# Five moves of work beside a dense feed-forward loop: an earlier load, later norm factors, later kernel products, and column tiles in turns

## The chip, the cores and the metric

The kernel runs on one core of a Trainium2 chip. The metric is the time on the device in microseconds (us). The engines are TensorE (PE; PEld is its weight load), VectorE (DVE), ScalarE (ACT), GpSimd (POOL, which here mostly issues transfers on a queue of its own) and SyncE (SP, which issues the transfers of the feed-forward weights).

## The reference

A block with adaptive layer norm: a diagonal state space convolution (S4D) over 2048 tokens of 576 channels, then a dense feed-forward layer with ReLU.

```python
def _A_ref(u, ...):                       # L = 2048 tokens, D = 576 channels, N = 128 states
    dt = jnp.exp(log_dt)
    A = -jnp.exp(log_A_real) + 1j * A_imag
    C = (C_real + 1j * C_imag) * dt[:, None]
    P = jnp.exp((A * dt[:, None])[:, :, None] * pos[None, None, :])
    K = 2.0 * jnp.einsum("dn,dnl->dl", C, P).real
    y = irfft(rfft(u_t, 2 * L) * rfft(K, 2 * L), 2 * L)[:, :, :L]
    return y + u * D_skip

def _B_ref(x, w1, w2):                    # 576 -> 4608 -> 576
    return jnp.maximum(x @ w1, 0) @ w2

mod = (silu(c) @ w_mod)                   # sa, ca, ga, sb, cb, gb
h = layernorm(x) * (1 + ca) + sa
x = x + ga * _A_ref(h, ...)
h = layernorm(x) * (1 + cb) + sb
x = x + gb * _B_ref(h, w1, w2)
```

## The kernel before

The 2048 tokens are cut into four blocks of 512. The convolution of block s needs spectra of the channels (`U`) and of the convolution kernel (`K`) of every block up to s; `Ud`, `Rd` and `Kd` are copies of them in device memory, and `Ua`, `R`, `Ka` are tiles that are loaded from there. The channels are worked in two halves p = 0 and 1.

Up to about 213 us a prelude makes the first part of the convolution kernel and runs convolution 0. Then one loop, `ffn`, carries the program: 144 groups g, 36 for each block of tokens. A group is 14 matmuls `hps` (`first(g)`, line 1305) and, two groups behind, 14 matmuls `acc` (`second`, line 1330). Between them ACT writes `hh`, the ReLU, and DVE writes `hl`, what is left of it for a second pass (line 1311). `hps` has two buffers, so `first(g + 2)` waits for `hl` of g. In block 0 the weights are also split (`w`, on ACT and DVE) and kept for the later blocks.

All other work runs beside that loop. `step()` is called four times a group; each call takes a few items from the generator of the current block. An item that yields a number is DVE work of about so many us, `None` is PE work, and `-1` ends the step. Block 0's generator makes the rest of the convolution kernel (`rest`: rotations `rots` on DVE into `W1r`, then matmuls `products` into `kps`, line 440, from three-block products with 48 columns and one-block products with 16) and, alternating with it, the first norm of block 1, then convolution 1. Block 1's generator finishes block 0's output, makes what the rest of the kernel needs (`rest` again, with 32 columns) and runs convolution 2; block 2's runs convolution 3.

Convolution s is written as a list of pieces, some of them alternating by `both`: transform `U` (`mm_U`, `spec_U`), transform the kernel (`mm_K`, `spec_K`: a butterfly into K, then K2 from K and the loaded R), multiply (`product`: Y from K2 with `Ua`, the spectrum of block 0, and from R with the own U), transform back (`back`, `inverse` into `ps_i`), then `norm2` with transposes `ps_t`, whose results `xh`, `xl`, `xs` are what the next block's `first` reads. Evictions `oT` free the accumulators of the block before. `cps`, the PSUM tile of `kps`, `ps_f` and `ps_i`, has one buffer in this part; spectra share a ring of six (`spec`).

The final order on each engine is set by a scheduler from this order of issue; each engine then works in order. POOL's queue takes saves and loads in the order in which they stand, and an entry that waits holds all behind it. The norm's `norms` makes the roots (variance to standard deviation, on ACT) and right behind them reciprocals and products on DVE.

Of the kernel before, what the change touches and what calls it, by code (L numbers as in the profile page):

```python
# [46 lines left out]
class KGen:  # L47
# [335 lines left out]
    def rest(self, psum, items, beside=iter(())):  # L383


        nc, k = self.nc, self.k
# [3 lines left out]
        with ExitStack() as ctx:  # L390
# [37 lines left out]
            def products(h, W1, W2, blocks):  # L428
                na = 16 * len(blocks)
                key = (h // 6, blocks)  # L430
                if key not in kes:
                    kes[key] = pt.tile([P, na, 72], F32, name=f"ker_{h}")
                ke = kes[key]
                for half in range(2):
                    ps = psum.tile([P, 6, na], F32, tag="cps", bufs=1, name="kps")
                    for q in range(6):
                        for dd in range(4):
                            ch = dd * 12 + 6 * half + q
                            for r in range(2):
                                nc.tensor.matmul(  # L440
                                    ps[32 * dd : 32 * dd + 32, q, :],
                                    W2[:, r, :, ch],
                                    W1[:, :na, r, ch],
                                    start=(r == 0),
                                    stop=(r == 1),
                                )
                        if q == 2:
                            yield None
                    q0 = 12 * (h % 6) + 6 * half
                    nc.scalar.activation(  # L450
                        ke[:, :, q0 : q0 + 6], ps.rearrange("p q a -> p a q"), AF.Copy
                    )
                    yield None
                rows[key] = rows.get(key, 0) + 1
                if rows[key] == 6:
                    yield -1
                    for i, s in enumerate(blocks):
                        self.store(
                            s, h // 6, ke[:, 16 * i : 16 * i + 16].rearrange("p a q -> p (a q)"),
                            nc.gpsimd,  # L460
                        )

            nxt = load(items[0][0])
            yield -1
            prev = iter(())
            for i, (h, blocks) in enumerate(items):
                W2, W0, Z = nxt
# [19 lines left out]
class Body:  # L487
# [317 lines left out]

    def norms(self, st, kept):

        nc = self.nc
        rs = []
        for i in range(4):  # L810
            mv = self.sm.tile([P, 5], F32, tag="mv", bufs=4, name="mv")
            nc.vector.bn_aggr(out=mv[:, 0:2], in_=st[i])
            sq = nc.scalar.activation(mv[:, 2:3], mv[:, 1:2], AF.Sqrt, bias=self.eps)
            if kept:
                self.tc.keep_in_program_order(sq)
            else:
                self.kept(sq)
            rs.append(mv)
        for mv in rs:
            nc.vector.reciprocal(mv[:, 3:4], mv[:, 2:3])  # L820
            nc.vector.tensor_scalar(
                mv[:, 4:5], mv[:, 0:1], mv[:, 3:4], -1.0, op0=ALU.mult, op1=ALU.mult
            )
        return rs

    def sums(self, name):
        return [self.sm.tile([P, 2, 6], F32, tag="st", bufs=8, name=name) for _ in range(4)]
# [11 lines left out]
    def norm1(self, x2, h):  # L839

        f = self.nc.vector.scalar_tensor_tensor
        st = self.sums("st1")
        for p in range(2):
            yield from self.stats(
                lambda i: x2[:, i, p * PC : (p + 1) * PC], [t[:, p] for t in st]
            )
        rs = self.norms(st, False)
        yield 2.0
        for i in range(4):
            mv = rs[i]  # L850
            f(h[:, i], x2[:, i], mv[:, 0:1], self.m["ca"], op0=ALU.subtract, op1=ALU.mult)
            f(h[:, i], h[:, i], mv[:, 3:4], self.m["sa"], op0=ALU.mult, op1=ALU.add)
            yield 1.6

    def conv(self, s):
# [33 lines left out]
        def spec_K(p, Z):  # L889
            R = self.load(self.Rd[s - 1][p], "R")  # L890
            Rs.append(R)
            K = self.spec(f"K_{s}_{p}")
            yield from self.butterfly(Z, K, -1)
            yield -1
            if s + 1 < NB:
                self.save(self.Rd[s][p], K)
# [10 lines left out]

        def product(p, Y):
            def pair(t):
                if t == 0 or s == 1:  # L910
                    Ka = (Rs if t else Ks)[p]
                else:
                    Ka = self.load(self.Kd[s - t][p], "Ka")
                Ua = Us[p] if t == s else self.load(self.Ud[t][p], "Ua")
                return Ka, Ua

            order = [0, s, *range(1, s)]
            nxt = pair(0)
            yield -1
            for i, t in enumerate(order):  # L920
                Ka, Ua = nxt
                if i + 1 < len(order):
                    nxt = pair(order[i + 1])
                yield from self.product(Y, Ka, Ua, i == 0)

# [6 lines left out]
            yield from self.butterfly(Y, V, 1)  # L932
            Vs.append(V)

        Us, Ks, Rs, Vs = [], [], [], []
        if s == 1:
            ZU = self.spec("Z")
            yield from mm_U(0, ZU)
# [3 lines left out]
            yield from both(spec_U(1, Z1), mm_K(0, ZK))  # L942
            kt[1] = self.load_kt(s, 1)
            yield from spec_K(0, ZK)
            ZK = self.spec("Z")
            Y = self.spec(f"Y_{s}_0")
            yield from both(product(0, Y), mm_K(1, ZK))
        else:
            ZK = self.spec("Z")
            yield from both(self.norm1(x2, h), mm_K(0, ZK))  # L950
# [610 lines left out]
```

## Time and profile before

| | us |
|---|---|
| three runs | 1371.61, 1366.92, 1363.95 |
| median | 1366.92 |
| profiled execution: its span | 1360.4 |
| PE busy in it | 1226.0 |
| DVE busy | 871.4 |
| ACT busy | 503.5 |
| prelude, up to the first groups | 213 |

The profiled execution has no time of its own beside its span; the median stands 6.5 us above that span. Rows of the trace give a start, a duration, the engine, the line, the operation and the tiles as out<-in; a bracket behind a row is the time that the engine stood idle before it and what ended that idle time. Rows of waits give the engine and line that waited, what for, and the total in us, the number of times and the longest. Line numbers are those of the kernel before.

### The profile page before, as it was taken

What the parts mean: (1) busy time and instruction counts of PE and PEld (TensorE: products, weight loads), DVE (VectorE), ACT (ScalarE), POOL (GpSimd) and SP (SyncE); (2) the same over time, 40 slices, a digit from 0 to 9 for tenths busy, and PEclk for the clock granted to TensorE, in tenths of its full rate; (3) what the DMA queues carried; (4) which work ended last, traced back from release to release, by engine and by line L of the source; (5) the groups of instructions that cost most, each with busy time, mean ns of one, the idle gap of its engine ahead of it and who ended that gap; (6) DMA issues with size and microseconds to landing.
All of it is one profiled execution on the core that took longest, in us unless ns stands there. A gap on an engine that the chain in (4) does not pass through costs nothing.

```text
span 1360.4 us, 26053 instructions
## 1 busy us (share of the span) xinstructions
PE 1226.0 (90%) x10608; PEld 973.7 (72%) x10608; DVE 871.4 (64%) x1351; ACT 503.5 (37%) x1014; POOL 195.3 (14%) x271
## 2 busy tenths in 40 slices
PE   5125797999999987999999999999999999999998
PEld 3124565777787766777777887787888888888886
DVE  5978997998878698469737986266999222111111
ACT  7986234222224311622233225333322253233321
POOL 1777231111120100021101100100010000000000
PEclk9557899999999998999999999999999999999999
DMA  6666499988898755699689894677997567666651
GB/s 196 243 246 241 135 356 366 331 292 275 292 344 289 265 199 207 205 362 316 236 278 342 294 362 143 206 245 233 317 348 259 178 177 211 198 195 197 197 174 61
DMA packets 132424, 340.47 MB, mean 250 GB/s; under 512 B 22352, under 2 KB 22672, under 8 KB 132304
## 3 DMA queue, kind: packets, MB, share of 16 engines
q1 hardware_dynamic: 105200, 215.21, 48.9%
q0 software_dynamic: 26816, 123.01, 24.6%
q8 instruction: 83, 1.36, 0.4%
q10 hardware_dynamic: 288, 0.59, 0.1%
q14 instruction: 37, 0.30, 0.1%
HBM read 258.55 MB, written 80.22 MB: 249 GB/s over the span
## 4 chain that ended last, share of the span: by engine, by line
PE 70%; DVE 11%; DMA 10%; issue 4%; ACT 2%; POOL 1%; SPq 0%; DVEq 0%; ACTq 0%; POOLq 0%
PE acc L1330 28%; PE hps L1305 28%; PE kps L440 5%; PE ps_f L757 4%; PE kps L262 3%; DVE T L509 2%; DVE Y L509 2%; DMA Ua<-Ud 2%; DMA Ud<-U 2%; DVE k L133 1%; PE ps_i L998 1%; DMA h<-in_x_dram 1%; DMA Ka<-Rd 1%; DMA Zr<-Zd 1%; DMA W1d<-W 1%
## 5 line engine op out<-in xcount | busy, mean ns | idle before, releaser
L1330 PE MATMUL acc<-hh,w 128*128 128x512 f32 x1296 | 422.1, 400 | 0.3 <-DVE w L509 0.3
L1305 PE MATMUL hps<-xh,w 128*128 128x512 f32 x1152 | 394.3, 402 | 4.4 <-ACT xh L1061 3.5
L1311 DVE SCALAR_TENSOR_TENSOR hl<-hps,hh 128x512 fp32r<-128x512 f32 x144 | 99.0, 688 | 291.3 <-ACT hh L1310 291.0
L1330 PEld LDWEIGHTS acc<-hh,w 128*128 128x128 f32 x1296 | 242.1, 188 | 52.5 <-DVE w L509 0.9
L1330 PE MATMUL acc<-hl,w 128*128 128x512 f32 x720 | 278.7, 399 | 0.0
L1305 PEld LDWEIGHTS hps<-xh,w 128*128 128x128 f32 x1152 | 217.4, 190 | 52.1 <-ACT xh L1061 4.7
L1305 PE MATMUL hps<-xl,w 128*128 128x512 f32 x576 | 230.8, 401 | 0.2 <-DVE xl L1066 0.2
L1310 ACT ACTIVATE hh<-hps 128x512 fp32r<-128x512 f32 x144 | 86.0, 598 | 354.6 <-PE hps L1305 347.0
L1283 ACT ACTIVATE w<-r 128x576 fp32r<-128x576 f32 x144 | 98.6, 686 | 217.9 <-issue 168.4
L1330 PEld LDWEIGHTS acc<-hl,w 128*128 128x128 f32 x720 | 135.3, 188 | 28.2
L1305 PEld LDWEIGHTS hps<-xl,w 128*128 128x128 f32 x576 | 109.2, 190 | 24.8 <-DVE xl L1066 1.5
L1305 PE MATMUL hps<-xs,w 128*128 128x512 f32 x288 | 97.2, 417 | 14.3 <-DVE hl L1311 14.0
L1276 ACT ACTIVATE w<-r 128x640 fp32r<-128x640 f32 x142 | 104.0, 733 | 12.4 <-DMA r<-in_w_dram 12.4
L262 PE MATMUL kps<-W,W 128*32 128x16 f32 x2304 | 40.3, 215 | 71.5 <-POOL W L59 47.3
L262 PEld LDWEIGHTS kps<-W,W 128*32 128x32 f32 x2304 | 37.9, 150 | 76.2 <-POOL W L59 49.7
L440 PEld LDWEIGHTS kps<-W1r,W2r 128*32 128x32 f32 x3456 | 68.4, 146 | 30.7 <-issue 16.8
L509 DVE TENSOR_TENSOR Y<-Y,T 128x1152 f32<-128x1152 f32 x64 | 84.7, 1351 | 0.2
L440 PE MATMUL kps<-W1r,W2r 128*32 128x48 f32 (+2 forms) x3456 | 77.4, 238 | 7.0 <-DVE W1r L412 3.3
L1305 PEld LDWEIGHTS hps<-xs,w 128*128 128x128 f32 x288 | 52.8, 190 | 28.3 <-DVE hl L1311 17.1
L758 ACT ACTIVATE Z<-ps_f 128x288 f32<-128x288 f32 x104 | 42.4, 407 | 63.1 <-PE ps_f L757 62.3
L509 DVE TENSOR_TENSOR w<-r,w 128x512 fp32r<-128x512 f32 (+2 forms) x108 | 57.9, 572 | 8.6 <-ACT w L1283 8.6
L509 DVE TENSOR_TENSOR W<-Z 128x576 f32<-128x576 f32 x52 | 37.1, 752 | 29.3 <-ACT Z L758 29.3
(216 smaller groups left out, 1362.8 us busy)
## 6 DMA issues: line engine op xcount, KB each, us to landing
r<-in_w_dram SPq DMA_DIRECT2D x144, 320.0 KB, 4.2
r<-in_w_dram SPq DMA_DIRECT2D x144, 288.0 KB, 3.7
w<-L1d SPq DMA_DIRECT2D x108, 320.0 KB, 3.0
w<-L2d SPq DMA_DIRECT2D x108, 288.0 KB, 3.2
W2r<-W2d POOLq DMA_DIRECT2D x18, 1536.0 KB, 9.4
W2d<-W SPq DMA_DIRECT2D x10, 1536.0 KB, 7.4
W<-W1d POOLq DMA_DIRECT2D x18, 768.0 KB, 8.9
Ua<-Ud POOLq DMA_DIRECT2D x12, 1152.0 KB, 10.3
```

The costliest lines, as they stand in the source:

```text
L133: self.nc.vector.scalar_tensor_tensor(f[:, i].rearrange(pair, u=2), th, float(slot), k[:, i].rearrange(pair, u=2), op0=ALU.mult, op1=ALU.s ...
L262: self.nc.tensor.matmul(ps[32 * dd : 32 * dd + 32, 12 * u + q, :], W2[:, r, :, ch], W1[:, u, :, r, ch], start=(r == 0), stop=(r == 1),)
L440: nc.tensor.matmul(ps[32 * dd : 32 * dd + 32, q, :], W2[:, r, :, ch], W1[:, :na, r, ch], start=(r == 0), stop=(r == 1),)
L509: return self.kept(self.nc.vector.tensor_tensor(*args, **kw))
L757: kept(nc.tensor.matmul(o, fc[:, n2, c, :], src(n2), start=True, stop=True))
L758: nc.scalar.activation(Z[:, n2, c], ps[:, :PC], AF.Copy)
L1276: nc.scalar.activation(w[:, 0], r, AF.Copy)
L1283: nc.scalar.activation(w[:, 0:D], r2[g], AF.Copy)
L1305: nc.tensor.matmul(ps, a, x, start=(i == 0), stop=(i == 13))
L1310: nc.scalar.activation(hh, ps, AF.Relu)
L1311: nc.vector.scalar_tensor_tensor(hl, ps, 0.0, hh, op0=ALU.max, op1=ALU.subtract)
L1330: nc.tensor.matmul(acc[i], a, x, start=(f == 0 and j in (0, 3, 6, 9, 12)), stop=(f == NF - 1 and j in (2, 5, 8, 11, 13)),)
```

## The change

Five pieces. The matmuls of `products` go through the four column tiles for one half of the sum, then for the other, where they finished a column tile before the next. In block 1 `rest` ends five steps behind its first load, where it ended one. `norms` is split into `roots` and `factors`; `norm1` has its factors three steps behind the roots. In convolution 1 `Ua` is loaded between the two parts of K's butterfly and kept in a list for the product. Also there, `Y` is allocated ahead of the tile for the next transform of the kernel, and that transform starts three items later beside the product.

```diff
@@ -434,9 +434,9 @@
                 for half in range(2):
                     ps = psum.tile([P, 6, na], F32, tag="cps", bufs=1, name="kps")
                     for q in range(6):
-                        for dd in range(4):
-                            ch = dd * 12 + 6 * half + q
-                            for r in range(2):
+                        for r in range(2):
+                            for dd in range(4):
+                                ch = dd * 12 + 6 * half + q
                                 nc.tensor.matmul(
                                     ps[32 * dd : 32 * dd + 32, q, :],
                                     W2[:, r, :, ch],
@@ -461,7 +461,8 @@
                         )
 
             nxt = load(items[0][0])
-            yield -1
+            for _ in range(1 if most == 48 else 5):
+                yield -1
             prev = iter(())
             for i, (h, blocks) in enumerate(items):
                 W2, W0, Z = nxt
@@ -805,6 +806,12 @@
 
     def norms(self, st, kept):
 
+        rs = self.roots(st, kept)
+        self.factors(rs)
+        return rs
+
+    def roots(self, st, kept):
+
         nc = self.nc
         rs = []
         for i in range(4):
@@ -816,12 +823,16 @@
             else:
                 self.kept(sq)
             rs.append(mv)
+        return rs
+
+    def factors(self, rs):
+
+        nc = self.nc
         for mv in rs:
             nc.vector.reciprocal(mv[:, 3:4], mv[:, 2:3])
             nc.vector.tensor_scalar(
                 mv[:, 4:5], mv[:, 0:1], mv[:, 3:4], -1.0, op0=ALU.mult, op1=ALU.mult
             )
-        return rs
 
     def sums(self, name):
         return [self.sm.tile([P, 2, 6], F32, tag="st", bufs=8, name=name) for _ in range(4)]
@@ -844,8 +855,12 @@
             yield from self.stats(
                 lambda i: x2[:, i, p * PC : (p + 1) * PC], [t[:, p] for t in st]
             )
-        rs = self.norms(st, False)
-        yield 2.0
+        rs = self.roots(st, False)
+        yield 1.0
+        for _ in range(3):
+            yield -1
+        self.factors(rs)
+        yield 1.0
         for i in range(4):
             mv = rs[i]
             f(h[:, i], x2[:, i], mv[:, 0:1], self.m["ca"], op0=ALU.subtract, op1=ALU.mult)
@@ -890,7 +905,11 @@
             R = self.load(self.Rd[s - 1][p], "R")
             Rs.append(R)
             K = self.spec(f"K_{s}_{p}")
-            yield from self.butterfly(Z, K, -1)
+            W = self.spec("W")
+            yield from self.butterfly1(Z, W)
+            if s == 1:
+                Uas.append(self.load(self.Ud[0][p], "Ua"))
+            yield from self.butterfly2(W, K, -1)
             yield -1
             if s + 1 < NB:
                 self.save(self.Rd[s][p], K)
@@ -911,7 +930,9 @@
                     Ka = (Rs if t else Ks)[p]
                 else:
                     Ka = self.load(self.Kd[s - t][p], "Ka")
-                Ua = Us[p] if t == s else self.load(self.Ud[t][p], "Ua")
+                if t == s:
+                    return Ka, Us[p]
+                Ua = Uas[p] if s == 1 else self.load(self.Ud[t][p], "Ua")
                 return Ka, Ua
 
             order = [0, s, *range(1, s)]
@@ -932,7 +953,7 @@
             yield from self.butterfly(Y, V, 1)
             Vs.append(V)
 
-        Us, Ks, Rs, Vs = [], [], [], []
+        Us, Ks, Rs, Vs, Uas = [], [], [], [], []
         if s == 1:
             ZU = self.spec("Z")
             yield from mm_U(0, ZU)
@@ -942,9 +963,9 @@
             yield from both(spec_U(1, Z1), mm_K(0, ZK))
             kt[1] = self.load_kt(s, 1)
             yield from spec_K(0, ZK)
+            Y = self.spec(f"Y_{s}_0")
             ZK = self.spec("Z")
-            Y = self.spec(f"Y_{s}_0")
-            yield from both(product(0, Y), mm_K(1, ZK))
+            yield from both(product(0, Y), after(3, mm_K(1, ZK)))
         else:
             ZK = self.spec("Z")
             yield from both(self.norm1(x2, h), mm_K(0, ZK))
```

On POOL's queue in convolution 1: `Ud_1` is the save of U's second half, `kt` a load of the convolution kernel, `Rd` and `Kd` the saves of K and K2, `R` and `Ua` loads. Before:

```order
L748 DMA Ud_1_104<-U_1_5469 128x4x576
L1238 DMA kt<-kd_1_60 128x16x72
L748 DMA Rd_0_111<-K_0_5563 128x4x576
L748 DMA Kd_0_115<-K_1_0_5615 128x4x576
L744 DMA Ua<-Ud_0_101 128x4x576
L744 DMA R<-Rd_1_110 128x4x576
L748 DMA Rd_1_112<-K_1_5846 128x4x576
L744 DMA Ua<-Ud_1_102 128x4x576
L748 DMA Kd_1_116<-K_1_1_5909 128x4x576
```

and after:

```order
L749 DMA Ud_1_104<-U_1_5496 128x4x576
L745 DMA Ua<-Ud_0_101 128x4x576
L1259 DMA kt<-kd_1_60 128x16x72
L749 DMA Rd_0_111<-K_0_5595 128x4x576
L749 DMA Kd_0_115<-K_1_0_5644 128x4x576
L745 DMA R<-Rd_1_110 128x4x576
L745 DMA Ua<-Ud_1_102 128x4x576
L749 DMA Rd_1_112<-K_1_5865 128x4x576
L749 DMA Kd_1_116<-K_1_1_5923 128x4x576
```

The load of `Ua` for half 0 moved from behind the saves `Rd_0` and `Kd_0` to right behind `Ud_1`; for half 1 it moved ahead of the save `Rd_1`.

On DVE at the same place, where the product of half 0 begins (`Y_0`; `K_1_0` is K2; `w` are splits of the feed-forward weights). Before:

```order
L1311 SCALAR_TENSOR_TENSOR hl<-hps,hh 128x512
L509 TENSOR_TENSOR w_5661<-r_5625,w_5661 128x640
L509 TENSOR_TENSOR w_5702<-r_5571,w_5702 128x64
L509 TENSOR_TENSOR w_5702<-r_5571,w_5702 128x512
L509 TENSOR_TENSOR Y_0_5647<-K_1_0_5615,Ua 128x4x288 x2
L509 TENSOR_TENSOR T<-K_1_0_5615,Ua 128x1152 x2
L509 TENSOR_TENSOR Y_0_5647<-Y_0_5647,T 128x4x288 x2
L1311 SCALAR_TENSOR_TENSOR hl<-hps,hh 128x512
L509 TENSOR_TENSOR T<-R,U_0_5378 128x1152 x2
```

and after:

```order
L918 SCALAR_TENSOR_TENSOR K_1_0_5644<-R,sgn,K_0_5595 128x4x288
L920 SCALAR_TENSOR_TENSOR K_1_0_5644<-R,sgn,K_0_5595 128x4x288
L1332 SCALAR_TENSOR_TENSOR hl<-hps,hh 128x512
L510 TENSOR_TENSOR Y_0_5667<-K_1_0_5644,Ua 128x4x288 x2
L510 TENSOR_TENSOR w_5684<-r_5555,w_5684 128x64
L510 TENSOR_TENSOR w_5684<-r_5555,w_5684 128x512
L510 TENSOR_TENSOR w_5658<-r_5623,w_5658 128x640
L510 TENSOR_TENSOR T<-K_1_0_5644,Ua 128x1152
L1332 SCALAR_TENSOR_TENSOR hl<-hps,hh 128x512
L510 TENSOR_TENSOR Y_0_5667<-Y_0_5667,T 128x4x288
L510 TENSOR_TENSOR T<-K_1_0_5644,Ua 128x1152
```

The first product moved ahead of three weight splits, which now stand between its pieces, and an `hl` stands in the midst of it.

On ACT at the end of block 0's groups (`oT` and `o` evict the accumulators; `xf`, `xs`, `xh` are the input of block 1's groups). Before:

```order
L1416 ACTIVATE oT<-acc_0_3035,m_gb 128x512
L1061 ACTIVATE xh_6180<-xf 128x512
L1059 ACTIVATE xf<-ps_t,m_sb,m_cb 128x512
L1416 ACTIVATE oT<-acc_0_3036,m_gb 128x512
L1061 ACTIVATE xh_6180<-xf 128x512
L1059 ACTIVATE xf<-ps_t,m_sb,m_cb 128x512
L1061 ACTIVATE xh_6180<-xf 128x512
L1059 ACTIVATE xf<-ps_t,m_sb,m_cb 128x512
L1061 ACTIVATE xh_6180<-xf 128x512
L1310 ACTIVATE hh<-hps 128x512
L1276 ACTIVATE w_6392<-r_6364 128x640
L1310 ACTIVATE hh<-hps 128x512
```

and after:

```order
L1437 ACTIVATE oT<-acc_0_3035,m_gb 128x512
L1082 ACTIVATE xs_6189<-xf 128x512
L1437 ACTIVATE oT<-acc_0_3036,m_gb 128x512
L1437 ACTIVATE oT<-acc_0_3037,m_gb 128x512
L1080 ACTIVATE xf<-ps_t,m_sb,m_cb 128x512
L1437 ACTIVATE oT<-acc_0_3038,m_gb 128x512
L1082 ACTIVATE xh_6187<-xf 128x512
L1080 ACTIVATE xf<-ps_t,m_sb,m_cb 128x512
L1437 ACTIVATE o_6452<-acc_0_3039,m_gb 128x512
L1082 ACTIVATE xh_6187<-xf 128x512
L1080 ACTIVATE xf<-ps_t,m_sb,m_cb 128x512
L1304 ACTIVATE w_6470<-r_6366 128x576
```

All five evictions now stand ahead of the last `xh`, of which two more follow; two did before.

On DVE at block 1's start, where the rotations for the kernel's rest begin (`x_0` is block 0's output). Before:

```order
L1477 TENSOR_TENSOR x_0_2525<-ps_o_6535,x_0_2525 128x64
L1311 SCALAR_TENSOR_TENSOR hl<-hps,hh 128x512
L408 TENSOR_TENSOR T<-W_6_6567,Zr_6568 128x1536
L410 TENSOR_TENSOR W1r_6585<-W_6_6567,Zr_6568 128x1536
L412 TENSOR_TENSOR W1r_6585<-W1r_6585,T 128x16x48
L414 TENSOR_TENSOR W1r_6585<-W1r_6585,T 128x16x48
L1311 SCALAR_TENSOR_TENSOR hl<-hps,hh 128x512
L408 TENSOR_TENSOR T<-W1r_6585,Zr_6568 128x1536
L410 TENSOR_TENSOR W1r_6585<-W1r_6585,Zr_6568 128x1536
L412 TENSOR_TENSOR W1r_6585<-W1r_6585,T 128x16x48
L414 TENSOR_TENSOR W1r_6585<-W1r_6585,T 128x16x48
L1311 SCALAR_TENSOR_TENSOR hl<-hps,hh 128x512
```

and after:

```order
L1498 TENSOR_TENSOR x_0_2525<-ps_o_6535,x_0_2525 128x64
L1332 SCALAR_TENSOR_TENSOR hl<-hps,hh 128x512
L408 TENSOR_TENSOR T<-W_6_6567,Zr_6568 128x1536
L410 TENSOR_TENSOR W1r_6628<-W_6_6567,Zr_6568 128x1536
L412 TENSOR_TENSOR W1r_6628<-W1r_6628,T 128x16x48
L1332 SCALAR_TENSOR_TENSOR hl<-hps,hh 128x512
L414 TENSOR_TENSOR W1r_6628<-W1r_6628,T 128x16x48
L408 TENSOR_TENSOR T<-W1r_6628,Zr_6568 128x1536
L410 TENSOR_TENSOR W1r_6628<-W1r_6628,Zr_6568 128x1536
L412 TENSOR_TENSOR W1r_6628<-W1r_6628,T 128x16x48
L414 TENSOR_TENSOR W1r_6628<-W1r_6628,T 128x16x48
L1332 SCALAR_TENSOR_TENSOR hl<-hps,hh 128x512
```

The rotations come one `hl` later against block 0's output, and an `hl` stands within the first of them.

## The prediction

> **What bounds the kernel now.** I read the page first: its busy shares and the chain that ended last.
>
> ```profile
> span 1360.4 us, 26053 instructions
> PE 1226.0 (90%) x10608; PEld 973.7 (72%) x10608; DVE 871.4 (64%) x1351; ACT 503.5 (37%) x1014; POOL 195.3 (14%) x271
> PE 70%; DVE 11%; DMA 10%; issue 4%; ACT 2%; POOL 1%; SPq 0%; DVEq 0%; ACTq 0%; POOLq 0%
> ```
>
> TensorE (PE) carries the end. What can be won without fewer matmuls is its idle time, and time at a low clock. Second I read busy time by stretches: from 445 to 560 us convolution 1 runs beside block 0's last groups, to 620 block 1 starts, and behind 852 block 2.
>
> ```profile
> core 0: us, PE busy (x) PEld busy (x) DVE busy (x) ACT busy (x) POOL busy (x), PEclk, DMA share, GB/s
> 230.00:445.00 215.00, 209.60 (x2945) 163.39 (x2944) 187.89 (x232) 58.14 (x115) 30.53 (x46) 1.00 0.87 309
> 445.00:560.00 115.00, 102.29 (x421) 79.45 (x420) 92.55 (x144) 34.89 (x64) 6.43 (x8) 0.96 0.63 216
> 560.00:620.00 60.00, 55.56 (x513) 43.51 (x512) 36.47 (x40) 20.40 (x35) 10.24 (x16) 0.97 0.88 314
> 852.00:1061.00 209.00, 209.00 (x916) 168.38 (x915) 148.59 (x193) 70.79 (x128) 14.57 (x20) 1.00 0.80 266
> ```
>
> PE idles 5.4 us in the first 215, where DVE is nearly as full, 12.7 in the next 115, 4.4 in the 60 behind, and nothing from 852 on. Third, who PE waits for: three rows of the wait view from 445 to 625 us, and the only one behind 625.
>
> ```profile
> PE hps L1305 <- DVE hl L1311: 12.4, 5, 4.8
> PE kps L440 <- DVE W1r L412: 3.3, 1, 3.3
> PE kps L440 <- ACT w L1283: 1.2, 1, 1.2
> PE ps_i L998 <- DVE V L509: 2.6, 1, 2.6
> ```
>
> `hps` has two buffers, so a group's first matmuls wait until VectorE (DVE) has written `hl` two groups back. DVE is in order: `hl` stands behind convolution 1's products. Fourth, the timeline, for what DVE itself waits for there.
>
> ```profile
> 453.12 1.41 DVE L901 SCALAR_TENSOR_TENSOR K<-R,sgn,K 128x1152 f32<-128x1152 f32 x1
> 460.62 0.83 DVE L509 TENSOR_TENSOR w<-r,w 128x64 fp32r<-128x64 f32 x2 [2.90 <-ACT w L1283]
> 466.45 2.63 DVE L509 TENSOR_TENSOR Y<-K,Ua 128x1152 f32<-128x1152 f32 x2 [5.01 <-DMA Ua<-Ud]
> 512.05 2.63 DVE L509 TENSOR_TENSOR Y<-K,Ua 128x1152 f32<-128x1152 f32 x2 [2.79 <-DMA Ua<-Ud]
> 440.73 0.76 POOL L748 DMA_DIRECT2D Ud<-U  x1 [8.96 <-DVE U L509]
> 455.57 0.75 POOL L744 DMA_DIRECT2D Ua<-Ud  x1
> 485.40 0.75 POOL L744 DMA_DIRECT2D R<-Rd  x1 [29.08 <-DVE T L509]
> 501.06 0.75 POOL L744 DMA_DIRECT2D Ua<-Ud  x1
> 455.57 10.76 DMA Ua<-Ud
> 501.06 10.90 DMA Ua<-Ud
> ```
>
> The last two rows are from the chain: start and length. Between 453 and 512 us DVE stands idle three times ahead of a product, 2.90 + 5.01 + 2.79 = 10.7 us, and two of these end with `Ua`, issued late on POOL's queue. PE pays for it some groups later, with its clock too:
>
> ```profile
> 524.95 1.22 PE L1305 MATMUL hps<-xs,w 128*128 128x512 f32 x2 [4.81 <-DVE hl L1311]
> 536.04 1.22 PE L1305 MATMUL hps<-xs,w 128*128 128x512 f32 x2 [2.81 <-DVE hl L1311]
> 524.90:528.40 3.50, 3.45 (x8) 2.77 (x9) 3.50 (x3) 0.00 (x0) 0.00 (x0) 0.51 0.00 0
> 535.20:542.00 6.80, 5.96 (x14) 4.56 (x15) 6.76 (x15) 0.00 (x0) 0.00 (x0) 0.50 0.57 188
> 600.00:603.50 3.50, 3.50 (x89) 3.02 (x82) 1.04 (x1) 0.35 (x1) 0.00 (x0) 0.51 1.05 391
> ```
>
> The granted clock is 0.51, 0.50 and 0.51 there, half of 1.00: 1.7, 3.4 and 1.7 us lost.
>
> **The change, part by part.**
>
> Part 1, `Ua` behind K's first butterfly half. It adds nothing; `Ua` of half 0 moves on POOL's queue from behind two saves to right behind the save of `Ud` (440.73), so it goes near 441.5 and, at 10.9 us, lands near 452.4, ahead of the end of K2 (453.12 + 1.41). Queued behind it are a `kt` load, which waited for PE until 446.35 anyway, and both saves: 0.75 us of issue on a queue that had been idle for 8.96. The order also takes Y's first product ahead of the three `w` splits (one ends the 2.90 idle). So the first two idles go, and the next thing late is DVE's own work. For half 1 `Ua` moves only ahead of one save, behind R; R's issue at 485.4 waited for a freed buffer, and I take it that much earlier as half 0 ends, about 8 us. Then `Ua` goes near 478 to 485 and lands by 496, while Y needs it near 501: the third idle goes too. DVE's chain is 10.7 us shorter at most. What PE can get back has its own bound: its five waits and the half clock of the first two stretches, 12.4 + 1.7 + 3.4 = 17.5 us; DVE's 10.7 binds first. Bounds 0 and 12.4; I take 10, nearest to the DVE rows, since a `w` split waits for ACT somewhere later, as the 2.90 shows.
>
> Part 2, K's transform three items later and `Y` allocated first. It costs no instruction. It belongs to the same order on DVE: K's butterfly of half 1 stands behind more of the product, and the inverse of half 1 then sits later against PE's groups. Three of its four matmul pairs stand behind the first part of block 0's last group instead of two. The tail up to block 1's first matmuls is a chain: inverse, norm, transposes, and on ACT and DVE this.
>
> ```profile
> 559.57 0.68 ACT L1416 ACTIVATE oT<-acc,m_gb 128x512 f32<-128x512 f32 x1
> 560.80 0.69 DVE L1066 TENSOR_TENSOR xl<-xf,xh 128x512 fp32r<-128x512 f32 x1 [2.28 <-ACT xh L1061]
> ```
>
> Before, two of five evictions of block 0's accumulators stand ahead of the last `xh`; after, all five: 3 × 0.68 = 2.0 us more on ACT. PE waited for nothing there before, so it is 0 if other matmuls still cover it, and 2.0 with a stretch of half clock, 3.4, is 5.4. I take +2, the ACT rows alone.
>
> Part 3, block 1's kernel products four steps, one group, later.
>
> ```profile
> 1338.87 3.17 PE hps L1305 x14
> 579.96 0.54 POOL L399 DMA_DIRECT2D Zr<-Zd  x1
> 588.22 1.76 DVE L408 TENSOR_TENSOR T<-W,Zr 128x1536 f32<-128x1536 f32 x1 [4.34 <-DMA Zr<-Zd]
> 597.48 0.96 DVE L412 TENSOR_TENSOR W1r<-W1r,T 128x768 f32<-128x768 f32 x1
> 598.50 0.31 PE L440 MATMUL kps<-W1r,W2r 128*32 128x32 f32 x2 [3.28 <-DVE W1r L412]
> ```
>
> The first row, from the chain, is half a group's matmuls without a wait. `Zr` goes and lands as before, since the loads stay ahead of the added steps; but DVE now has an `hl` first. PE wanted the product at 598.50 − 3.28 = 595.2; one group of 28 matmuls later is 595.2 + 2 × 3.17 = 601.5. DVE's two rotations took 588.22 to 598.44, 10.2 us; begun behind an `hl` near 590.2 they end near 600.4, 1.1 us in hand. So the wait of 3.28 and the half clock of 600 to 603.5 go: 5.0. Ends 0 (the wait moves along) and 6.2 (the wait of 1.2 goes too); I take 4, for the thin margin. Everything else of block 1 follows three to four steps later, with its queue order kept but for a `W2r` and a `Zr` that swap.
>
> Part 4, norm factors three steps behind their roots. Same instructions. Three steps are 4.8 us; norm1's DVE rows had an idle of their own in block 0:
>
> ```profile
> DVE mv L820 <- ACT mv L813: 5.8, 3, 5.5
> 418.17 0.75 PE L757 MATMUL ps_f<-h,fcU 128*128 128x288 f32 x2 [0.34 <-ACT Z L758]
> ```
>
> DVE waited 5.5 for a root; `hl` and `w` splits now go ahead of it. PE waited 0.34 at the transform that uses the result, so nothing is won; cover gone, it costs up to 4.8. I take 0. In convolution 2 the last inverse moves 1.5 groups later against PE, DVE's chain about one; of the wait of 2.6 between 0 and 2.6 goes, and the late tail may give as much back at the block's end. I take −1.
>
> Part 5, product matmuls by column tile in turns. 3456 matmuls, none fewer.
>
> ```profile
> 391.57 2.35 PE L440 MATMUL kps<-W1r,W2r 128*32 128x48 f32 x94
> 400.61 1.66 PE L440 MATMUL kps<-W1r,W2r 128*32 128x16 f32 x94
> 642.84 1.68 PE L440 MATMUL kps<-W1r,W2r 128*32 128x32 f32 x96
> 206.39 2.22 PE L632 MATMUL mps_gb<-wm_gb,cb 128*32 128x128 f32 x50 [1.53 <-DVE mv L821]
> ```
>
> 16 and 32 columns cost the same, some 17 ns each, so columns don't set their pace and the order need not either. The 48-column ones, 1152 in block 0, take 0.69 us more per 94; L632 goes in turns already and passes 128 columns at 2.22/50 = 44 ns with its single-tile rest. If turns bring 48 columns to the others' pace, 1152/94 × 0.69 = 8.5 us; if starts already overlap all that they can, 0; a loss is not excluded, 2. I take 4, half way: PE is the bound there (209.6 of 215), but DVE at 187.9 gives part back. A rule speaks against any gain: the Trainium skill ("TensorE: Matmul & The Clock Gate", Part 3) has weight loads overlap running matmuls only where the row group differs, and these four tiles share all rows; by it the sum has 0 here and ends at 1354. The trace doesn't agree: in the row of 600 to 603.5 PE is busy for 3.50 and weight loads for 3.02 of 3.5 us. The same page (Part 1) has the clock fall after idle of about 3.4 us; here 2.81 us, 10 behind a 4.81, was enough.
>
> The sum: −10 + 2 − 4 − 1 − 4 = −17 us. The profiled execution spans 1360.4, 6.5 under the median of 1366.92; against its own span 1343.4, and for the median 1349.9.
>
> **The rivals.**
>
> Given back. The `hl` waits are DVE's work, not `Ua`: DVE is busy 92.55 of 115 us, and with the idles gone its pieces may pile up elsewhere, with ACT's `w` splits between the products. If only the 5.01 goes, PE gets 5, the boundary takes 2, block 1's wait moves along and turns give 0 to 1: −3, 1364. For it speaks that 2.90 ended with ACT, not with a DMA; against it, that DVE ran without a gap behind 466 and PE's waits followed.
>
> Turns price each matmul. A pass round four tiles may cost more than two matmuls in a tile, because the sums of all four stay open at once; then all 3456 pay. At what the 48-column ones pay over the narrow, 0.69/94 = 7.3 ns, it is 25 us: 1366.9 − 13 + 25 = 1379, slower. It decides from (13 + 6.8)/3456 = 5.7 ns each on. L632's 44 ns, the one row in turns, speaks for it; against it, its columns are 128, which is likely what it pays for.
>
> Turns in full. The 8.5 us come and block 1's 6.2: −10 + 2 − 6.2 − 1 − 8.5 = −24, 1343. The Trainium skill ("TensorEngine Tiling (Array Packing)", Performance Considerations) gives each matmul some 60 cycles whatever its few columns, which would put 48 at the price of 16; the rows above have 2.35 against 1.66 before the change.
>
> **How the numbers follow.** Chances: forecast 0.62, given back 0.17, turns in full 0.14, turns priced 0.07. 0.5% (6.8 us) is about what a measurement can tell from no change. Faster: 0.62 + 0.14 + a little of the second less a little of the first, 0.76; same 0.17; slower 0.07. The likeliest is 1350, its own range 1342 to 1358; with the two neighbours 1339 to 1364.
>
> **What would show it.** Right: no `Y` wait on `Ua` between 445 and 560, `hl` waits there down from 12.4 to about 4, no half clock at 536, no kps wait of 3 us in block 1, 94 48-column products under 2.1 us. Wrong: a new wait of `hps` on `xh` or `xl` at block 1's start above 4 us, or 16-column products above 1.8.

## The result, and the profile after

The changed kernel takes 1351.05 us, the median of 6 runs (1348.62 to 1352.87), against 1367.59 for the kernel before (6 runs, 1363.95 to 1372.61). The ratio is 0.9896 (95% interval 0.9869 to 0.9922): 1.0% faster. The profiled execution took 1350.32 us and spans 1348.5; the prediction was 1350, against the median. In every run whose span is on record the time is some 1.8 us above it, so the profiled execution of before, which spans 1360.4, stands for an estimated 1362.2 us, 5 under the median of its kernel.

The page of the changed kernel. Its lines are numbered some 21 higher behind the new functions: L1326 is L1305 of before, L1332 L1311, L1351 L1330, L1019 L998, L510 L509.

```profile
span 1348.5 us, 26042 instructions
PE 1227.2 (91%) x10608; PEld 974.3 (72%) x10608; DVE 870.4 (65%) x1351; ACT 504.1 (37%) x1014; POOL 195.6 (15%) x271
```

PE's work is the same (1226.0 before); its idle time is 13 us shorter. The rows of waits of PE from 445 to 625 us, and the one from 625 to 900:

```profile
PE acc L1351 <- DVE w L510: 2.0, 1, 2.0
PE hps L1326 <- DVE hl L1332: 1.4, 1, 1.4
PE hps L1326 <- ACT xh L1082: 0.4, 1, 0.4
PE hps L1326 <- DVE xs L1085: 0.2, 1, 0.2
PE ps_i L1019 <- DVE x L510: 4.0, 1, 4.0
```

The `hl` waits of 12.4 us became 1.4 and a wait of 2.0 for a `w` split; both `kps` waits of block 1 are gone. New is the last row, 4.0 us in convolution 2 at 773 us. The same part of the timeline as before, on POOL and DVE:

```profile
442.78 0.75 POOL L745 DMA_DIRECT2D Ua<-Ud  x1
457.02 1.42 DVE L920 SCALAR_TENSOR_TENSOR K<-R,sgn,K 128x1152 f32<-128x1152 f32 x1
458.95 2.62 DVE L510 TENSOR_TENSOR Y<-K,Ua 128x1152 f32<-128x1152 f32 x2
485.39 0.75 POOL L745 DMA_DIRECT2D Ua<-Ud  x1 [5.93 <-DVE W L510]
502.57 1.35 DVE L510 TENSOR_TENSOR Y<-K,Ua 128x1152 f32<-128x1152 f32 x1
```

`Ua` is issued at 442.8 (455.6 before) and the first product follows K2 and one `hl` without a gap; that of half 1 starts at 502.6 with no bracket either. And the clock:

```profile
521.70:530.50 8.80, 7.26 (x19) 5.18 (x20) 8.80 (x17) 0.00 (x0) 0.00 (x0) 0.61 0.43 144
600.00:603.50 3.50, 3.50 (x100) 2.77 (x102) 3.29 (x5) 1.46 (x3) 1.31 (x2) 1.00 1.05 395
773.20:780.20 7.00, 6.96 (x18) 5.35 (x19) 3.61 (x4) 0.23 (x1) 3.66 (x5) 0.56 0.83 269
```

Of the stretches at half clock in block 0 one is left, block 1's is gone, and a new one of 7 us follows the new wait, at 0.56.

How long PE took between the first matmuls of two groups tells the place of every microsecond. The table is worked out from their starts in each kernel's trace, in us; group 20 stands at convolution 1's transforms, 35 is block 0's last, 41 to 50 hold block 1's kernel products, 50 to 75 convolution 2 and the door to block 2.

| kernel | start of 0 | 0 to 20 | 20 to 35 | 35 to 41 | 41 to 50 | 50 to 75 | 75 to 143 | 20 to 75 |
|---|---|---|---|---|---|---|---|---|
| before | 212.6 | 193.3 | 139.3 | 46.6 | 89.2 | 193.9 | 463.7 | 469.0 |
| changed | 214.8 | 192.2 | 127.9 | 46.3 | 82.2 | 198.8 | 464.6 | 455.2 |
| e1 Ua alone | 214.7 | 196.9 | 129.0 | 46.6 | 89.4 | 193.5 | 464.5 | 458.4 |
| e2 convolution 1 | 217.0 | 192.5 | 129.7 | 44.8 | 89.0 | 197.3 | 463.8 | 460.8 |
| e3 rest alone | 212.5 | 199.0 | 139.2 | 46.6 | 82.7 | 199.5 | 464.5 | 468.0 |
| e4 turns alone | 216.5 | 192.8 | 139.4 | 46.6 | 88.8 | 194.5 | 464.6 | 469.3 |
| e5 no rest | 213.9 | 192.3 | 127.3 | 46.3 | 88.7 | 196.7 | 464.4 | 459.0 |
| e6 no norm | 217.9 | 193.0 | 130.4 | 44.8 | 82.1 | 197.8 | 463.5 | 455.2 |
| e7 no turns | 215.9 | 198.0 | 127.1 | 46.4 | 84.4 | 197.2 | 464.1 | 455.1 |
| e8 inverse later | 213.8 | 194.7 | 127.3 | 46.3 | 84.2 | 197.5 | 464.2 | 455.3 |
| e9 inverse 5 | 216.5 | 192.2 | 127.7 | 46.4 | 83.6 | 201.1 | 463.8 | 458.8 |
| e10 inverse 5, room 8 | 220.5 | 191.1 | 127.6 | 46.3 | 90.5 | 191.4 | 464.9 | 455.7 |
| e11 inverse 5, rest 3 | 218.9 | 193.5 | 127.1 | 46.4 | 89.1 | 191.6 | 464.0 | 454.2 |
| e12 inverse 3 | 214.3 | 197.7 | 127.9 | 46.4 | 82.3 | 197.3 | 463.7 | 453.8 |

The first two columns scatter by 8 us each whatever was changed: group 0 starts between 212.5 and 220.5, and its first 20 groups take 191.1 to 199.0. From group 75 on all agree within 1.4, and between 20 and 75 kernels that share a piece agree within about 2, save for the waits told below. So the pieces are read there, and the whole from the ratios. Each line is one profiled execution of its kernel, and a boundary between groups is no fixed amount of work: before, 8 matmuls of convolution 1's inverse stand behind the start of group 35, in the changed kernel 12, in e2 and e6 none. From 20 to 41 all kernels do the same work.

### The profile page after: what moved, and what is told of

It reads as the page before. It is cut to its first block, busy times and chain, and to the rows that moved or that the text cites. A ratio compares the mean times of both kernels' runs of the same rounds, so it can differ in the third digit from the quotient of the medians.

```text
span 1348.5 us, 26042 instructions
## 1 busy us (share of the span) xinstructions
PE 1227.2 (91%) x10608; PEld 974.3 (72%) x10608; DVE 870.4 (65%) x1351; ACT 504.1 (37%) x1014; POOL 195.6 (15%) x271
## 5 line engine op out<-in xcount | busy, mean ns | idle before, releaser
L1351 PE MATMUL acc<-hh,w 128*128 128x512 f32 x1296 | 422.6, 400 | 2.1 <-DVE w L510 2.0
L1326 PE MATMUL hps<-xh,w 128*128 128x512 f32 x1152 | 395.9, 404 | 1.2 <-ACT xh L1082 1.2
L1351 PEld LDWEIGHTS acc<-hh,w 128*128 128x128 f32 x1296 | 243.8, 189 | 55.6 <-DVE w L510 2.8
L1351 PE MATMUL acc<-hl,w 128*128 128x512 f32 x720 | 279.9, 399 | 0.0
L1332 DVE SCALAR_TENSOR_TENSOR hl<-hps,hh 128x512 fp32r<-128x512 f32 x144 | 99.3, 689 | 279.8 <-ACT hh L1331 279.6
L1326 PEld LDWEIGHTS hps<-xh,w 128*128 128x128 f32 x1152 | 217.2, 190 | 49.7 <-ACT xh L1082 3.3
L1326 PE MATMUL hps<-xl,w 128*128 128x512 f32 x576 | 231.1, 401 | 0.6 <-DVE xl L1087 0.6
L1351 PEld LDWEIGHTS acc<-hl,w 128*128 128x128 f32 x720 | 135.8, 189 | 28.3
L1326 PEld LDWEIGHTS hps<-xl,w 128*128 128x128 f32 x576 | 109.2, 190 | 25.6 <-DVE xl L1087 2.2
L1326 PE MATMUL hps<-xs,w 128*128 128x512 f32 x288 | 98.2, 421 | 2.9 <-DVE hl L1332 2.7
L510 DVE TENSOR_TENSOR Y<-Y,T 128x1152 f32<-128x1152 f32 x64 | 85.0, 1356 | 0.1
L440 PEld LDWEIGHTS kps<-W1r,W2r 128*32 128x32 f32 x3456 | 64.4, 146 | 26.8 <-issue 20.2
L440 PE MATMUL kps<-W1r,W2r 128*32 128x48 f32 (+2 forms) x3456 | 73.4, 238 | 3.9 <-issue 3.9
L1326 PEld LDWEIGHTS hps<-xs,w 128*128 128x128 f32 x288 | 53.6, 192 | 16.0 <-DVE hl L1332 4.2
L510 DVE TENSOR_TENSOR W<-Z 128x576 f32<-128x576 f32 x52 | 37.1, 756 | 40.9 <-ACT Z L759 40.9
L510 DVE TENSOR_TENSOR w<-r,w 128x512 fp32r<-128x512 f32 (+2 forms) x108 | 58.4, 580 | 3.0 <-ACT w L1304 3.0
```

The costliest lines, as they stand in the source:

```text
L440: nc.tensor.matmul(ps[32 * dd : 32 * dd + 32, q, :], W2[:, r, :, ch], W1[:, :na, r, ch], start=(r == 0), stop=(r == 1),)
L510: return self.kept(self.nc.vector.tensor_tensor(*args, **kw))
L1326: nc.tensor.matmul(ps, a, x, start=(i == 0), stop=(i == 13))
L1332: nc.vector.scalar_tensor_tensor(hl, ps, 0.0, hh, op0=ALU.max, op1=ALU.subtract)
L1351: nc.tensor.matmul(acc[i], a, x, start=(f == 0 and j in (0, 3, 6, 9, 12)), stop=(f == NF - 1 and j in (2, 5, 8, 11, 13)),)
```

## The experiments

**e1, the earlier load of Ua alone.**

```diff
+            W = self.spec("W")
+            yield from self.butterfly1(Z, W)
+            if s == 1:
+                Uas.append(self.load(self.Ud[0][p], "Ua"))
+            yield from self.butterfly2(W, K, -1)
...
+                Ua = Uas[p] if s == 1 else self.load(self.Ud[t][p], "Ua")
```

> The kernel before with the earlier load of Ua alone. Theory (DVE's waits for Ua set the end of block 0): both Y waits on Ua in convolution 1 (5.0 and 2.8 us) go, the hl waits of PE there fall from 12.4 to 5 or less, and the run ends 7 to 10 us earlier, at 1358 to 1361. Rival (the order of the pieces sets it, not the load): the DVE wait is refilled by the w splits, hl waits stay above 9, and the gain is under 3 us, 1365 or more.

Ratio 0.9928 (0.9899 to 0.9957), a median of 1355.1 against 1365.18. Its waits of PE from 445 to 625:

```profile
PE kps L440 <- DVE W1r L412: 3.6, 1, 3.6
PE hps L1311 <- DVE hl L1317: 3.2, 2, 2.8
PE kps L440 <- ACT w L1289: 1.1, 1, 1.1
PE acc L1336 <- DVE w L509: 1.0, 1, 1.0
```

and, on DVE, what is left of the three idles of 10.7 us ahead of the products:

```profile
464.56 2.63 DVE L509 TENSOR_TENSOR Y<-K,Ua 128x1152 f32<-128x1152 f32 x2 [1.03 <-DMA Rd<-K]
```

The `hl` waits fall from 12.4 to 3.2 and groups 20 to 35 take 129.0 for 139.3 us: 10.3 less, all but 1.1 of what the whole change wins there. Of the 10.3, 8.4 are idle time of PE; the rest is matmuls that take less long, at a mean granted clock of 0.97 for 0.96. The rival, that the order of the pieces counts and not the load, falls. `kps` waits as before. And the gain is kept: group 62 starts 4.3 us earlier and DVE ends convolution 2's first inverse input 4.4 us earlier, so groups 50 to 75 take 193.5 for 193.9.

**e2, all of the change in convolution 1.** As e1, and:

```diff
-            ZK = self.spec("Z")
             Y = self.spec(f"Y_{s}_0")
-            yield from both(product(0, Y), mm_K(1, ZK))
+            ZK = self.spec("Z")
+            yield from both(product(0, Y), after(3, mm_K(1, ZK)))
```

> The kernel before with the earlier Ua, Y allocated ahead and the kernel's second transform three items later: all of the change in convolution 1. Theory: at most 2 us more than the earlier Ua alone, 1356 to 1360. Rival (the order of the pieces is what counts): 5 us or more beyond the earlier Ua alone.

Ratio 0.9942 (0.9911 to 0.9974), not to be told from e1's. By groups, against e1, it wins 1.1 us from 20 to 41 (174.5 for 175.6), and gives back 3.8 in convolution 2 (197.3 for 193.5), where PE waits 1.1 us at the first inverse and 3.0 at the last. Added to the earlier load, the order of these pieces is worth nothing.

**e3, block 1's products four steps later, alone.**

```diff
-            yield -1
+            for _ in range(1 if most == 48 else 5):
+                yield -1
             prev = iter(())
```

> The kernel before with block 1's kernel products four steps later alone. Theory: the kps waits of 3.3 and 1.2 us at block 1's start and the half clock behind them go, 5 to 6 us; convolution 2's end keeps its ps_i wait of 2.6 or less: 1361 to 1363. Rival one: the wait moves along, 1367. Rival two: the delay is what makes PE wait at convolution 2's first inverse (4.0 us in the changed kernel), so that wait is here too and takes the gain back, 1365 to 1368.

Ratio 1.0003 (0.9972 to 1.0035). The theory had the place right: groups 41 to 50 take 82.7 for 89.2, 6.5 less, and PE waits for nothing from 560 to 700 us. The second rival had the end right: groups 50 to 75, with convolution 2, take 199.5 for 193.9. Its waits of PE from 755 to 860:

```profile
PE ps_i L999 <- DVE x L510: 2.9, 1, 2.9
PE ps_i L999 <- DVE V L510: 2.7, 1, 2.7
```

The wait of 2.9 at convolution 2's first inverse is new; the last had one of 2.6 before. Of the 5.6 us lost there 3.1 are idle time, and 2.5 are matmuls that take longer, at a granted clock of 0.99 for 1.00 over these groups.

**e4, column tiles in turns, alone.**

```diff
-                        for dd in range(4):
-                            ch = dd * 12 + 6 * half + q
-                            for r in range(2):
+                        for r in range(2):
+                            for dd in range(4):
+                                ch = dd * 12 + 6 * half + q
```

> The kernel before with the column tiles in turns alone. Theory from the changed kernel's trace (a group with 192 products of 48 columns takes 11.25 us in place of 11.46): 0.2 us for each 192, 1.3 us for the 1152, less for the narrow ones: 1365 to 1367. Rival one, as in the prediction's upper bound: 8.5 us, 1359. Rival two, a cost for each matmul: 1370 or more.

Ratio 1.0017 (0.9990 to 1.0045). Rows of the view by groups for line 440 (busy time and mean ns, then the idle time ahead), this kernel first and the kernel before second, then a timeline row of this kernel for 16 columns:

```profile
L440 PE MATMUL kps<-W1r,W2r 128*32 128x48 f32 (+2 forms) x3456 | 73.8, 238 | 9.3 <-issue 4.4 <-DVE W1r L412 3.7 <-ACT w L1283 1.2
```

```profile
L440 PE MATMUL kps<-W1r,W2r 128*32 128x48 f32 (+2 forms) x3456 | 77.4, 238 | 7.0 <-DVE W1r L412 3.3 <-issue 2.5 <-ACT w L1283 1.2
```

```profile
404.12 1.47 PE L440 MATMUL kps<-W1r,W2r 128*32 128x16 f32 x88
```

PE is busy 3.6 us less: 24.3 ns each for 48 columns in rows of 88 (25.0 before, in rows of 94) and 16.7 for 16 (17.7). These rows are not of one length, though: where a matmul of the feed-forward breaks into a product, the old order has 2 matmuls ahead of it and 94 behind, the turns 8 and 88. Three rows of the kernel before, then three of this one:

```profile
390.39 0.36 PE L440 MATMUL kps<-W1r,W2r 128*32 128x48 f32 x2
391.57 2.35 PE L440 MATMUL kps<-W1r,W2r 128*32 128x48 f32 x94
394.75 2.33 PE L440 MATMUL kps<-W1r,W2r 128*32 128x48 f32 x96
```

```profile
394.08 0.38 PE L440 MATMUL kps<-W1r,W2r 128*32 128x48 f32 x8
395.29 2.14 PE L440 MATMUL kps<-W1r,W2r 128*32 128x48 f32 x88
398.25 2.30 PE L440 MATMUL kps<-W1r,W2r 128*32 128x48 f32 x96
```

Unbroken, 96 take 2.30 for 2.33 us, 0.3 ns each; broken, they take 2.52 for 2.71. Most of the gain is that 8 matmuls in turns pass in about the time of 2 in the old order. But PE waits 2.3 us more ahead of them, and groups 0 to 20 take 192.8 for 193.3. Neither the 8.5 us of the upper bound nor a cost for each matmul came.

**e5, the changed kernel without the four steps.**

```diff
-            for _ in range(1 if most == 48 else 5):
-                yield -1
+            yield -1
```

> The changed kernel without the four later steps in block 1. Theory: block 1's first groups lose their 6 to 7 us again (kps waits of 3.3 and 1.2, half clock), and convolution 2 gives back some of the 3.5 that it lost in the changed kernel, as it lost 5.5 where the four steps stood alone: 1352 to 1356. Rival (the four steps are worth nothing in this company either, as alone): 1351. Second rival: the four steps are what PE waits for in convolution 2, and without them it ends earlier, 1347.

Ratio 0.9921 (0.9896 to 0.9946). Groups 41 to 50 take 88.7 again, with a `kps` wait of 4.5 us; groups 50 to 75 take 196.7, 2.1 less than in the changed kernel. In this company the four steps are worth 6.5 − 2.1 = 4.4 us by the groups, where alone they were worth 6.5 − 5.6 = 0.9; the ratios here (0.9921 and 0.9896) have intervals that overlap. The 196.7 is still 2.8 above the kernel before, without the four steps.

**e6, the changed kernel without the later norm factors.**

```diff
-        rs = self.roots(st, False)
-        yield 1.0
-        for _ in range(3):
-            yield -1
-        self.factors(rs)
-        yield 1.0
+        rs = self.norms(st, False)
+        yield 2.0
```

> The changed kernel without the norm factors three steps behind. Theory: nothing in block 0, since DVE's wait for the root has cover; in convolution 2 the inverse comes 0.7 groups earlier against PE while DVE's chain does not, so the ps_i waits stay or grow: 1351 to 1356. Rival: the three steps cause the 4.0 us wait at convolution 2's first inverse; without them it goes with its half clock, 7 us: 1344 to 1347.

Ratio 0.9916 (0.9888 to 0.9943). Convolution 2 keeps most of its loss (197.8 for 198.8 and 193.9), with `ps_i` waits of 2.8 and 1.5 us: the rival, that these three steps cause the 4.0, falls. Groups 20 to 35 take 130.4 for 127.9, groups 35 to 41 44.8 for 46.3, which with convolution 2 is 2.5 − 1.5 − 1.0 = 0: from group 20 to 75 both take 455.2. The three steps are worth nothing there; the ratios, with intervals of 0.5%, don't tell them apart either.

**e7, the changed kernel without turns**: e4's edit the other way round.

> The changed kernel without the column tiles in turns. Theory: kps matmuls busy 77.4 in place of 73.8 us, but PE waits for DVE in the same groups, so of the 3.6 us at most 2 are lost: 1351 to 1353. Rival: all of it, 1355.

Ratio 0.9919 (0.9878 to 0.9960), against 0.9896 with turns, inside each other's intervals. Line 440 is busy 77.5 us, and from group 20 to 75 it takes 455.1 for 455.2. Block 1's products take 84.4, but they do so with turns too where PE waited 1 to 2 us there (e8, 84.2). Behind group 20 turns are worth nothing; ahead of it the scatter hides what they may be worth, and between e4's interval and the two ratios here it stays open between nothing and some 3 us.

**e8, the inverse later among the pieces.**

```diff
-            yield from both(spec_K(1, ZK), after(3, inverse(0, Vs[0])))
+            yield from both(spec_K(1, ZK), after(3 if s == 1 else 6, inverse(0, Vs[0])))
```

> The changed kernel with the inverse of half 0 in convolutions 2 and 3 begun six items after the kernel's spectrum in place of three, so that its adds stand behind less DVE work when PE comes to its second pair. Theory: the ps_i wait of 4.0 us at convolution 2's first inverse and the half clock behind it go, 7 us: 1343 to 1346. Rival: the product of half 1 begins later by what the inverse was moved, and PE waits at the last inverse instead: 1350 to 1353.

Ratio 0.9895 (0.9867 to 0.9923), no better. The wait of 4.0 became one of 3.1 us, one group later.

**e9 to e11, the inverse of half 0 in convolution 2 held back by whole steps**, with edits of e10 and of e11 below:

```diff
+def pause(n, g):
+    for _ in range(n):
+        yield -1
+    yield from g
...
-            yield from both(spec_K(1, ZK), after(3, inverse(0, Vs[0])))
+            yield from both(spec_K(1, ZK), after(3, pause(5 if s == 2 else 0, inverse(0, Vs[0]))))
...
-            room = (9.0, 7.0, 7.0, 7.0)[g // NF] - sum(recent[-3:])
+            room = (9.0, 8.0, 7.0, 7.0)[g // NF] - sum(recent[-3:])
...
-            for _ in range(1 if most == 48 else 5):
+            for _ in range(1 if most == 48 else 4):
```

> The changed kernel with the inverse of half 0 in convolution 2 five steps later, 1.07 groups against PE at its second pair (64.11 for 63.04 groups). Theory (convolution 2's chain on DVE is late against PE, so PE must be given other work until its adds are done): the ps_i wait of 4.0 and its half clock go, 7 us; the transposes then end at group 72.04, at block 2's door, and up to 4 us of new wait of hps on xh or xl come there: 1344 to 1349. Rival: what goes at the first inverse comes back whole at the last one or at the door: 1351 to 1353.

> As the one with the inverse five steps later, and with more DVE work allowed for each group of block 1 (8 for 7 in the steps' budget), which lets convolution 2's pieces come a group earlier: the last transposes end at 70.54. Theory: the first inverse waits 0 to 2 us, no wait at block 2's door: 1343 to 1347. Rival (DVE's chain does not come earlier with the issue): waits of 3 us or more at the inverses: 1349 to 1353.

> As the one with the inverse five steps later, with block 1's kernel products three steps later in place of four. Theory: the kps wait at block 1's start is 0.5 us or less still, the last transposes end at 71.50 and PE waits under 1 us at block 2's door: 1343 to 1346. Rival: one step less brings the kps wait back, 2 us or more, with the half clock behind it: 1349 or more.

e9, five steps: 0.9928 (0.9904 to 0.9952), worse by the groups: 50 to 75 take 201.1. Its timeline on DVE and PE:

```profile
791.27 1.36 DVE L510 TENSOR_TENSOR Y<-K,Ua 128x1152 f32<-128x1152 f32 x1 [7.97 <-DMA Ua<-Ud]
792.55 0.45 DVE L510 TENSOR_TENSOR x<-ps_i,x 128x288 f32<-128x288 f32 x1
793.05 2.29 PE L1019 MATMUL ps_i<-V,gc 128*128 128x288 f32 x4 [6.74 <-DVE x L510]
```

The third add came to stand behind the next product, which waits 7.97 us for its `Ua`; PE's next pair needs the one buffer that this add frees. e10, with more DVE work allowed a group (8 for 7): 0.9913 (0.9883 to 0.9943); groups 50 to 75 take 191.4, without a `ps_i` wait in convolution 2, but 41 to 50 90.5, with a `kps` wait of 4.0 us. e11, five steps and the products three steps later: 0.9892 (0.9861 to 0.9924); groups 50 to 75 take 191.6 and 41 to 50 89.1, with a wait of 3.5 us ahead of the products for something that the trace does not name. In both, PE came to convolution 2 later.

**e12, three steps, all adds ahead of the product**: `pause(3 if s == 2 else 0, ...)`, without the edits of e10 and e11.

> The changed kernel with the inverse of half 0 in convolution 2 three steps later, 0.46 groups against PE at its second pair (63.50 for 63.04 groups), and all of its adds on DVE ahead of the next product, which five steps later they were not. Theory: the ps_i wait of 4.0 at the first inverse falls to 1 us, under the length that brought the half clock: groups 61 to 72 take 80 to 82 us (86.8 in the changed kernel), and the run ends 4 to 6 us earlier, at 1345 to 1347, if block 1's products wait for no transfer. Rival: the wait stays above 2.5 us with its half clock, or comes back at the last inverse: 1350 or more.

Ratio 0.9929 (0.9901 to 0.9957). The first inverse does what the theory said: 0.4 us of wait, groups 61 to 66 in 36.6 for 43.0 us. Then PE waits at the last one:

```profile
813.31 0.73 PE L1326 MATMUL hps<-xs,w 128*128 128x512 f32 x2 [0.81 <-DVE hl L1332]
821.52 0.73 PE L1326 MATMUL hps<-xs,w 128*128 128x512 f32 x2 [1.57 <-DVE hl L1332]
826.81 1.21 PE L1019 MATMUL ps_i<-V,gc 128*128 128x288 f32 x4 [1.60 <-DVE V L510]
```

Groups 66 to 75 take 72.6 for 67.7 us: of the 6.4 won at the first inverse, 4.9 are given back by the last, and 41 to 75 take 279.5 for 281.0. The 4 to 6 us of the theory did not come. None of the kernels tried is shown to be faster than the changed one.

## Why the prediction was right, and where its steps were not

The total was right, −17 predicted and −16.5 between the medians. The two profiled spans differ by 11.9 only: the execution of before was quicker than all six runs behind the median, and group 0, ahead of which nothing was changed, starts 2.2 us later in the changed one. Of the signs set down, no wait of `Y` for `Ua`, the fall of the `hl` waits, full clock at 536 and no `kps` wait in block 1 came; the price of the 48-column products did not. The terms, by groups:

**Part 1, −10: right in place and size.** The load alone gives −10.3 (e1). The bound that I took for it, DVE's three idles of 10.7 us, held there; 1.03 of them is left. One reason was off: that a `w` split would wait for ACT later. In the changed kernel DVE waits 0.3 us for a `w` of ACT's; the longest idle, 3.39 us, is ahead of K's butterfly, for a transform that ACT evicts.

```profile
449.47 1.43 DVE L510 TENSOR_TENSOR W<-Z 128x576 f32<-128x576 f32 x2 [3.39 <-ACT Z L759]
```

**Part 2, the boundary, +2: a loss that did not come.** Block 0's last group takes 15.15 us for 13.46, but not for ACT's evictions: PE is busy for 15.0 of them, with 12 matmuls of the inverse where it had 8. For ACT and DVE it waits 0.4 and 0.2 us at block 1's start, and 35 to 41 take 46.3 for 46.6. The term ought to have been 0, the end of the range at which other matmuls cover the evictions.

**Part 3, −4: right mechanism, too small, and with the wrong reason for its margin.** In the changed kernel groups 41 to 50 take 7.0 us less, the far end of 6.2 and some of the turns. I had let the rotations begin behind an `hl`, without DVE's wait for `Zr`:

```profile
572.56 0.69 DVE L1332 SCALAR_TENSOR_TENSOR hl<-hps,hh 128x512 fp32r<-128x512 f32 x1 [3.41 <-ACT hh L1331]
577.39 1.76 DVE L408 TENSOR_TENSOR T<-W,Zr 128x1536 f32<-128x1536 f32 x1 [4.14 <-DMA Zr<-Zd]
587.65 0.95 DVE L414 TENSOR_TENSOR W1r<-W1r,T 128x768 f32<-128x768 f32 x1
590.86 1.65 PE L440 MATMUL kps<-W1r,W2r 128*32 128x32 f32 x96
```

It waits 4.14 us, as before (4.34). What changed against them is that PE comes a group later: both rotations are done at 588.6 and PE wants them at 590.86, 2.3 us in hand where I had 1.1.

**Part 4 and convolution 2, −1: the wrong sign, +4.9.** This is the step that failed. I reckoned with the last inverse alone, and there it came as forecast: it stands at group 69.9 for 68.5, and its wait of 2.6 is gone. The first inverse, which I left out, moved by 0.7 groups only (63.1 for 62.4). And I counted in groups, and forgot that groups had become shorter: from group 41 to 62 PE takes 176.6 us for 183.3, while DVE ends the inverse's input V 185.5 us behind the start of group 41, for 179.4 before. In all, PE came 17.3 us earlier to group 62, and DVE ended V only 4.6 us earlier (763.83 for 768.39, rows of 2.90 us each). Nothing of part 3 shortened DVE's work in between.

```profile
763.83 2.90 DVE L510 TENSOR_TENSOR V<-W 128x576 f32<-128x576 f32 x6
769.91 2.90 DVE L510 TENSOR_TENSOR K<-W 128x576 f32<-128x576 f32 x6
772.72 0.46 DVE L510 TENSOR_TENSOR x<-ps_i,x 128x288 f32<-128x288 f32 x1
773.24 2.29 PE L1019 MATMUL ps_i<-V,gc 128*128 128x288 f32 x4 [3.99 <-DVE x L510]
```

PE did its first pair, and the second waits for the buffer, which the add frees; the add stands behind the next K's butterfly. In place of the old wait of 2.6 came one of 3.99 with 7 us at clock 0.56 behind it. The second V ends 3.8 us earlier (821.7 for 825.5). Not all of the 4.9 is part 3's: 2.8 stays without the four steps (e5), and the pieces of convolution 1 alone lose 3.4 there (e2); what in them does it was not tried. From group 41 to 75 all fourteen kernels take 280 to 286 us, wherever the inverse stands and whether block 1's start waits or not (before 283.1, changed 281.0, e3 282.2, e12 279.5). That is mostly PE's own work: it is busy for 275 to 278 of them in every kernel, and only 4.0 to 8.4 us of idle time change their place. The waits at the inverses all end with DVE's `x` or `V`, which speaks for DVE's chain as the limit there; in e10 and e11, where PE comes later, they are gone, and PE idles ahead of block 1's products in their place. No run made DVE's chain shorter, so this cause is argued and not shown.

**Part 5, −4: the size of the matmul time was right, its worth was not.** Busy time fell by 3.6 us alone and 4.0 in the changed kernel (73.4). But it fell as much at 16 columns (1.5 us in e4) as at 48 (1.5), and mostly where products are broken into: 24.3 ns is still far from 16.7, so a bound of 2.1 us for 94 of them was not met. And e4 shows no gain at the end, less than 1.4 us by its interval.

So the sum came out as −11.4 up to group 35, −0.3, −7.0 and +4.9, which is −13.8 from group 20 to 75: what parts 1 to 3 won beyond their terms (1.4, 2.3 and 3.0) paid for the larger part of what convolution 2 (5.9) and the turns (4) fell short. That the total came so near is in part luck. The interval of the ratio, −17.9 to −10.7 us, holds both −13.8 and the −16.5 of the medians.

**The rivals.** "Given back" named the mechanism that fits best, DVE's work, at the wrong place: not in block 0, but in convolution 2, and for 4.9 us. Neither price of the turns showed.

**The clock.** Waits of 2.0 and 1.4 us that follow each other were enough for 0.61, the 3.99 for 0.56; e12's waits of 0.81, 1.57 and 1.60, 5 to 8 us apart, left it at 1.00 over 786 to 843.5. By the Trainium skill ("TensorE: Matmul & The Clock Gate", Part 1) the clock falls after about 3.4 us of idle; the trace agrees for the single wait of 3.99 and for the sum of the neighbouring 2.0 and 1.4, neither of which reaches it alone.

## What to carry to other kernels

Find the engine that is in order and late, sum the idles that late transfers bring it, and move those transfers ahead of saves in their queue: the sum of the idles, 10.7 us, bounded the gain of that move alone, and 10.3 of it came. A wait that is taken away on the bound engine alone makes it arrive early at the next thing that the other engine must finish, so follow the times of both engines, not their places in the order, to the next meeting before the gain is booked. Pieces that are worth little alone can be worth several microseconds beside others (the four steps, 0.9 and 4.4 us by the groups of single executions), so a change is tried both by adding each part and by leaving it out.

## What was not expected of the hardware

The first 20 groups, the same work in all these kernels, take 191.1 to 199.0 us, and in the whole program PE idles 2.5 (before) to 8.3 us (e11) ahead of the kernel products without a cause that the profile names; the runs of one kernel differ by up to 20 us (1355.74 to 1375.5 in 31 runs of the kernel before). Four column tiles in turns gained 0.3 ns a matmul in unbroken rows, so the order within a tile had cost next to nothing there: at 48 columns some 24 ns each remain either way of going round. Weight loads overlap matmuls among column tiles that share all 128 rows: in 391.57 to 393.86 of before, line 440 alone has 2.15 us of loads within 2.29 us of matmuls. And 8 matmuls round the tiles, begun behind a matmul of 512 columns, took 0.38 us where 2 in one tile took 0.36.
